# Splitting the first 256-token block of the feed-forward part, and rounding its weights earlier, in a fused top-k attention and SwiGLU kernel

## The chip, the cores and the metric

The kernel runs on one core of a Trainium2 chip. The metric is the device time of one execution in microseconds; the time before is the median of three runs. The profile is of one execution, taken by the hardware profiler. Its engines: PE (matrix multiply; PEld is its weight load), DVE, ACT, POOL, and SP, which here only issues DMAs.

## The reference

Attention over 8 batches x 8 heads, 576 tokens of 64 elements, in which each query keeps its 32 largest scores; then a gated feed-forward layer (512 to 1536 to 512) over all 4608 tokens. The three weight matrices lie in memory as 8-byte numbers; the kernel loads them as pairs of 32-bit words and makes fp32 of them itself.

```python
scores = scale * np.matmul(q, k.transpose(0, 1, 3, 2))
kth = np.partition(scores, -top_k, axis=-1)[..., -top_k:-top_k + 1]
scores = np.where(scores >= kth, scores, -1000000000.0)
attn = np.exp(scores - max); attn = attn / (sum + 1e-09)
x = np.matmul(attn, v)            # then (B,H,S,D) -> (4608, 512)
g = x @ w_gate
silu = g * (1.0 / (1.0 + np.exp(-g)))
return (silu * (x @ w_val)) @ w_out
```

## The kernel before, in words

**Units.** Attention is cut into 160 units (`units`, L227): batch, query tile of 128 tokens (five per batch, the last of 64), pair of heads. Four units, one per head pair, finish one query tile. Every fifth group of four is a short one ("J" below: `units[n][1] == J`, units 16 to 19, 36 to 39 and so on), with half the work. The loop at L514 is software-pipelined over units: in its pass n, DVE selects the top 32 of unit n (`select`, L257: four rounds of MAX8, L270, and three of MATCH_REPLACE8, L274, then the mask, L280), PE makes the scores of unit n+1 (`scores`, L234), turns the weights of unit n-1 (`turn`, L317) and multiplies unit n-2 by its values (`values`, L338). Unit n below means pass n of that loop, and it begins with the first MAX8 on `sc`.

**Order.** The order of each engine's instructions is exactly the order in which this Python text emits them (L570 to L583 add a dependency from each to the one before it). So an instruction that waits holds back all that was emitted behind it on its engine.

**Feed-forward blocks.** `values` copies its result into `xT[kb]`, a block of 256 tokens, and counts in `done`. When a block is full, `feed` (L396) turns it into pieces: 24 calls of eight matmul records each (`product`, L404 to L419; a call is one of 12 row groups of the gate or of the value matrix; each fp32 matmul shows as two records), then 12 calls of four records each for the second matmul (L440 to L460). After every second call of `product`, ACT and POOL instructions are queued (`gate`, `value`) and flushed later. That makes 36 pieces a block, 18 blocks, 648 pieces. A block of 256 tokens is full after eight ordinary units, so block 0 can start in pass 9 (the values of unit 7 come in pass 9), block 1 in pass 17.

**Credit.** `pieces(n)` (L493) emits up to n pieces, if a block is full and there is credit. Each pass adds 4.6 credits (2.3 in a J pass), capped at 8; a piece costs 1. A pass calls pieces(2), (1), (1), (1) and (6), at fixed places between the attention's instructions. After the loop, `while piece()` (L564) emits what is left.

**Rounding.** `weights` (L135) cuts the three weight matrices into 72 tiles of 128x256. Step k of this generator, in this order, finishes tile k-5 (DVE, L130), works on tile k-4 (DVE L120 and L123, then POOL L127), begins tile k-3 (POOL L108, ACT L113 and L115) and starts the load of tile k (SP, L102). There are 77 steps. `rounding(m)` emits m steps; `need(n)` (L160), called before matmuls, emits steps until n tiles are finished. Before the loop three steps are emitted. In the loop, each pass emits rounding(2) (rounding(1) from pass 10), then (1), (1), (1), at four places between the DVE's rounds of selection; so five steps a pass, four from pass 10 on.

Of the kernel before, what the change touches and what calls it, by code (L numbers as in the profile page):

```python
# [8 lines left out]
AF = mybir.ActivationFunctionType  # L9
# [6 lines left out]
P = 128  # L16
# [4 lines left out]
BLK = 256  # L21
# [6 lines left out]
def kernel(  # L28
# [27 lines left out]
    nc = tc.nc  # L56
    B, H, S, D = q.shape
    DM, DFF = w_gate.shape
    J = S // P
    JP = J * P  # L60
    R = S - JP
    NHP = H // 2
    KC = DM // P
    MC = DFF // P
    MS = MC // 2
    NBLK = B * S // BLK
    scale = 1.0 / float(D) ** 0.5
    assert D == 64 and R == 64 and H * D == DM and DM == 512 and B * S % BLK == 0

# [86 lines left out]
    def rounding(n):  # L156
        for _ in range(n):
            next(weight, None)

    def need(n):  # L160

        while ready[0] < n:
            next(weight)
# [63 lines left out]
    units = [(b, qt, hp) for b in range(B) for qt in range(J + 1) for hp in range(NHP)]  # L227
# [105 lines left out]
                yield  # L333
        state[n]["et"] = et

    xT, done = {}, {}

    def values(n):  # L338

        b, qt, hp = units[n]  # L340
        vt, v_last, vl = vs[b * NHP + hp]
        et = state.pop(n)["et"]
        last = qt == J
        ql = R if last else P
        av = ps_t.tile([P, P], FP32, tag="t", name="av")
        if not last:
            nc.tensor.matmul(av[:], vl[:], et[:, J, :], start=True, stop=False)
        for c in range(J + 1 if last else J):
            kl = R if c == J else P
            for hh in range(2):  # L350
                moving = (
                    et[0:kl, c, hh * R : (hh + 1) * R]
                    if last
                    else et[:, c + hh * (J + 1), :]
                )
                nc.tensor.matmul(  # L356
                    av[hh * R : (hh + 1) * R, 0:ql],
                    v_last[:, hh, :] if c == J else vt[:, hh, c, :],
                    moving,
                    start=last and c == 0,  # L360
                    stop=c == (J if last else J - 1),
                )
        c0 = b * S + qt * P
        at = c0
        while at < c0 + ql:
            kb = at // BLK
            n_c = min((kb + 1) * BLK, c0 + ql) - at
            if kb not in xT:
                xT[kb] = ffn.tile([P, NHP, BLK], FP32, tag="xT", name="xT", bufs=3)
                done[kb] = 0  # L370
            nc.scalar.copy(  # L371
                xT[kb][:, hp, at - kb * BLK : at - kb * BLK + n_c],
                av[:, at - c0 : at - c0 + n_c],
            )
            done[kb] += n_c
            at += n_c

    def store(o, g0):

        at = g0  # L380
        while at < g0 + P:
            b, c = divmod(at, S)
            j, p0 = divmod(c, P)
            n = min(g0 + P - at, S - c, P - p0)
            r0 = b * S + (c if j == J else J * p0 + j)
            dst = out[r0 : r0 + n, :] if j == J else out[r0 : r0 + J * (n - 1) + 1 : J, :]
            nc.sync.dma_start(dst, o[at - g0 : at - g0 + n, :])
            at += n

    on_act, on_pool = [], []  # L390

    def flush(queue):
        while queue:
            queue.pop(0)()

    def feed(kb):  # L396

        x = xT.pop(kb)
        hs = []

        def product(w, s, then):  # L404
            ps = ps_f.tile([P, 2, BLK], FP32, tag="f", name="f")
            need(8 * s + (4 if w is wg else 8))
            for i in range(2):
                m = 2 * s + i
                for c in range(KC):
                    nc.tensor.matmul(  # L410
                        ps[:, i, :],
                        w[:, c, m * P : (m + 1) * P],
                        x[:, c, :],
                        start=(c == 0),
                        stop=(c == KC - 1),
                    )
                if i == 1:
                    on_act.append(lambda: then(ps))
                yield  # L419

        for s in range(MS):
            h = ffn.tile([P, 2, BLK], FP32, tag="h", name="h", bufs=MS + 1)
            hs.append(h)


            def gate(ps, h=h):
                half = ffn.tile([P, 2, BLK], FP32, tag="gv", name="half_g", bufs=3)
                nc.scalar.activation(h[:], ps[:], AF.Tanh, scale=0.5)  # L428
                nc.scalar.mul(half[:], ps[:], 0.5)
                nc.scalar.add(h[:], h[:], 1.0)  # L430
                on_pool.append(lambda: nc.gpsimd.tensor_mul(h[:], h[:], half[:]))  # L431

            def value(ps, h=h):
                val = ffn.tile([P, 2, BLK], FP32, tag="gv", name="val", bufs=3)
                nc.scalar.copy(val[:], ps[:])  # L435
                on_pool.append(lambda: nc.gpsimd.tensor_mul(h[:], h[:], val[:]))  # L436

            yield from product(wg, s, gate)
            yield from product(wv, s, value)
        for t in range(BLK // P):  # L440
            ps = ps_f.tile([P, DM], FP32, tag="f", name="o_ps")
            for m in range(MC):
                need(8 * MS + 2 * m + 2)
                nc.tensor.matmul(  # L444
                    ps[:],
                    hs[m // 2][:, m % 2, t * P : (t + 1) * P],
                    wo[:, m, :],
                    start=(m == 0),
                    stop=(m == MC - 1),
                )  # L450
                if m == MC - 1:

                    def finish(ps=ps, t=t):
                        o = ffn.tile([P, DM], FP32, tag="o", name="o")
                        nc.scalar.copy(o[:], ps[:])
                        store(o, kb * BLK + t * P)

                    on_act.append(finish)
                if m % 2 == 1:
                    yield  # L460

    NU = len(units)
    todo = list(range(NBLK))
    current = []

    def piece():

        if len(on_act) > 1:
            flush(on_act)
        if len(on_pool) > 1:  # L470
            flush(on_pool)
        while True:
            if not current:
                if not todo or done.get(todo[0], 0) < NHP * BLK:
                    return False
                flush(on_act)
                flush(on_pool)
                current.append(feed(todo.pop(0)))
            if next(current[0], 0) == 0:
                current.pop()  # L480
                continue
            return True

    def fetch(n):

# [5 lines left out]
            load(i + NHP)  # L491

    def pieces(n):  # L493
        for _ in range(n):
            if credit[0] >= 1 and piece():
                credit[0] -= 1

    def run(steps):
        for _ in steps:
# [12 lines left out]
    credit = [0.0]  # L512
    no = iter(())
    for n in range(NU + 3):  # L514
        on = 0 <= n < NU
        was = 0 <= n - 1 < NU
        first = n < 2 * NHP + 2
        topk = select(n) if on else no
        over = normalize(n - 1) if was else no
        nxt = scores(n + 1) if n + 1 < NU else no  # L520
        over_et = turn(n - 1) if was else no
        ahead = fetch(n + 2) if n + 2 < NU else no
        if on:
            credit[0] = min(credit[0] + (2.3 if units[n][1] == J else 4.6), 8.0)
        flush(on_act)
        if was:
            penalize(n - 1)
            weigh(n - 1)
        flush(on_pool)
        if 0 <= n - 2 < NU:  # L530
            values(n - 2)
            b, qt, hp = units[n - 2]
            if qt == J and b + 1 < B:
                load_v((b + 1) * NHP + hp)
        next(topk, None)
        next(topk, None)
        rounding(2 if first else 1)
        next(topk, None)
        next(topk, None)
        rounding(1)  # L540
        pieces(2)
        next(over, None)
        flush(on_act)
        next(over, None)
        flush(on_pool)
        next(nxt, None)
        next(topk, None)
        rounding(1)
        pieces(1)
        next(nxt, None)  # L550
        flush(on_act)
        flush(on_pool)
        next(over_et, None)
        pieces(1)
        next(over_et, None)
        next(topk, None)
        rounding(1)
        next(topk, None)
        next(topk, None)
        next(ahead, None)  # L560
        pieces(1)
        next(ahead, None)
        pieces(6)
    while piece():  # L564
        pass
# [48 lines left out]
```

## Time and profile before

| what | number |
|---|---|
| median of three runs (lowest to highest) | 2067.86 us (2063.32 to 2073.43) |
| the profiled execution: its time, its span | 2063.52 us, 2061.4 us |
| PE busy, share of the span | 1854.4 us, 90% |
| DVE busy | 1673.8 us, 81% |
| ACT, POOL busy | 1150.5 us, 777.8 us |
| chain that ended last: PE, DVE, ACT | 77%, 11%, 6% |

The page cuts the span into 40 slices of about 51.5 us and gives the busy tenths of each engine in each. The trace answers for any stretch how long each engine was busy in it, with the granted PE clock (1.00 is full), and lists instructions in order of time with what ended the idle time before each.

### The profile page before, as it was taken

Reading aid. Unit: us, or ns where it says so; the run is one execution under the profiler, and the core shown is the slowest. Engines: PE = TensorE matmul, PEld = TensorE weight load, DVE = VectorE, ACT = ScalarE, POOL = GpSimd, SP = SyncE. Lnnn points to the kernel's source line nnn. Section 1 sums busy time; section 2 is a strip of 40 time slices with the busy share of each in tenths; the row PEclk is TensorE's granted clock in tenths of the full one; section 3 lists DMA queues with packets and bytes.
Section 4 is the critical chain, followed back from the end, with each engine's and each line's share of the span. In section 5 each row is a group of like instructions: output and inputs, shape, how many; then the busy total and the mean of one; then the engine's idle time right before and its main releaser. Section 6 shows DMA issues by size and latency. Waiting matters only on the chain.

```text
span 2061.4 us, 28952 instructions
## 1 busy us (share of the span) xinstructions
PE 1854.4 (90%) x9888; PEld 1276.5 (62%) x9888; DVE 1673.8 (81%) x3712; ACT 1150.5 (56%) x2565; POOL 777.8 (38%) x686
## 2 busy tenths in 40 slices
PE   3447779979999998899999999999999998999999
PEld 1325536657576766475757675757576766575756
DVE  5998986898789987989788987898788997989710
ACT  3555555656565655565656565656565655565621
POOL 2555543325333533242424342424333433242412
PEclk9657989989999999999999999999999999999999
DMA  5321111100020001100030002100020001000000
GB/s 149 88 77 62 62 33 49 33 6 1 19 64 11 1 13 43 38 1 11 9 74 1 11 2 58 24 11 1 19 64 11 1 12 42 17 1 11 1 11 11
DMA packets 111251, 59.55 MB, mean 29 GB/s; under 512 B 89088, under 2 KB 97280, under 8 KB 111104
## 3 DMA queue, kind: packets, MB, share of 16 engines
q1 hardware_dynamic: 111104, 57.70, 10.5%
q8 instruction: 79, 1.29, 0.3%
q14 instruction: 68, 0.56, 0.1%
HBM read 48.23 MB, written 9.44 MB: 28 GB/s over the span
## 4 chain that ended last, share of the span: by engine, by line
PE 77%; DVE 11%; ACT 6%; issue 3%; POOL 2%; SPq 1%; DMA 0%; POOLq 0%; DVEq 0%; ACTq 0%
PE f L410 35%; PE o_ps L444 18%; PE av L356 7%; PE etps L327 6%; PE s L250 5%; DVE m L270 4%; DVE rest L274 3%; ACT et L328 2%; PE s L251 2%; PE kqps L219 2%; DVE bits L123 1%; ACT e L315 1%; PE s L242 1%; DVE e L280 1%; POOL bits L127 1%
## 5 line engine op out<-in xcount | busy, mean ns | idle before, releaser
L270 DVE MAX8 m<-rest 128x8 f32<-128x576 f32 x864 | 613.6, 748 | 2.2
L292 POOL TENSOR_TENSOR e<-e,sc 128x1152 f32<-128x1152 f32 (+1 forms) x160 | 382.1, 2388 | 422.9 <-DVE e L280 307.7
L274 DVE MATCH_REPLACE8 rest<-m,rest 128x576 f32<-128x576 f32 x576 | 424.5, 745 | 0.0
L410 PE MATMUL f<-xT,wg 128*128 128x256 f32 x1728 | 413.0, 387 | 5.4 <-ACT xT L371 5.4
L444 PE MATMUL o_ps<-wo,h 128*128 128x512 f32 x864 | 407.5, 605 | 8.5 <-DVE wo L130 8.5
L410 PE MATMUL f<-xT,wv 128*128 128x256 f32 x1728 | 412.2, 385 | 0.0
L410 PEld LDWEIGHTS f<-xT,wg 128*128 128x128 f32 x1728 | 318.7, 192 | 57.4 <-issue 10.9
L410 PEld LDWEIGHTS f<-xT,wv 128*128 128x128 f32 x1728 | 321.5, 192 | 43.5 <-issue 3.4
L327 PE MATMUL etps<-ident,e 128*128 128x128 f32 (+1 forms) x1312 | 211.2, 290 | 132.2 <-issue 85.9
L431 POOL TENSOR_TENSOR h<-h,half_g 128x512 f32<-128x512 f32 x108 | 138.7, 1284 | 474.4 <-ACT h L430 474.4
L328 ACT COPY et<-etps 128x512 f32<-128x512 f32 (+1 forms) x448 | 196.3, 480 | 209.8 <-PE etps L327 209.7
L327 PEld LDWEIGHTS etps<-ident,e 128*128 128x128 f32 (+1 forms) x1312 | 164.8, 147 | 210.2 <-issue 136.3
L270 DVE MAX8 m<-sc 128x8 f32<-128x576 f32 x288 | 205.8, 752 | 85.7 <-ACT sc L246 42.0
L301 ACT ACTIVATE e<-e,bias 128x576 f32<-128x576 f32 x288 | 221.4, 773 | 81.3 <-POOL e L292 81.3
L444 PEld LDWEIGHTS o_ps<-wo,h 128*128 128x128 f32 x864 | 153.2, 192 | 150.2 <-issue 137.8
L436 POOL TENSOR_TENSOR h<-h,val 128x512 f32<-128x512 f32 x108 | 138.8, 1285 | 236.6 <-ACT val L435 236.3
L315 ACT ACTIVATE e<-e,tot 128x576 f32<-128x576 f32 x288 | 209.0, 771 | 19.2 <-DVE tot L312 19.2
L274 DVE MATCH_REPLACE8 rest<-m,sc 128x576 f32<-128x576 f32 x288 | 212.2, 745 | 0.0
L356 PE MATMUL av<-et,v 128*64 128x128 f32 (+1 forms) x2560 | 199.9, 284 | 8.7 <-ACT et L328 4.5
L356 PEld LDWEIGHTS av<-et,v 128*64 128x64 f32 x2560 | 150.7, 146 | 45.1 <-ACT et L328 22.6
L428 ACT ACTIVATE h<-f 128x512 f32<-128x512 f32 x108 | 64.4, 596 | 166.7 <-PE f L410 166.4
L250 PE MATMUL s<-kqT 64*128 64x512 f32 x512 | 153.1, 676 | 2.0 <-ACT kqT L224 2.0
(51 smaller groups left out, 1517.5 us busy)
## 6 DMA issues: line engine op xcount, KB each, us to landing
kq_in<-in_k_dram SPq DMA_DIRECT2D x64, 128.0 KB, 2.8
kq_in<-in_q_dram SPq DMA_DIRECT2D x64, 128.0 KB, 2.9
v<-in_v_dram SPq DMA_DIRECT2D x32, 256.0 KB, 3.1
w<-in_moe_w_gate_dram SPq DMA_DIRECT2D x24, 256.0 KB, 2.7
w<-in_moe_w_val_dram SPq DMA_DIRECT2D x24, 256.0 KB, 2.7
w<-in_moe_w_out_dram SPq DMA_DIRECT2D x24, 256.0 KB, 2.5
out_dram<-o SPq DMA_DIRECT2D x40, 128.0 KB, 2.4
out_dram<-o SPq DMA_DIRECT2D x16, 256.0 KB, 2.3
```

The costliest lines, as they stand in the source:

```text
L250: nc.tensor.matmul(ps[:, 1024 * hh : 1024 * hh + JP], slab[d, qs], slab[d, 0:JP])
L270: nc.vector.max(m[:, t, 8 * r : 8 * r + 8], cur[:, hs])
L274: nc.vector.match_replace(rest[:, hs], m[:, t, 8 * r : 8 * r + 8], cur[:, hs], LOWEST)
L292: nc.gpsimd.tensor_tensor(e[:, every], e[:, every], sc[:, every], ALU.add)
L301: nc.scalar.activation(e[:, hs], e[:, hs], AF.Exp, bias=bias[:, t : t + 1], scale=scale, accum_out=tot[:, t : t + 1],)
L315: nc.scalar.mul(e[:, hs], e[:, hs], tot[:, t : t + 1])
L327: nc.tensor.transpose(ps[0:kl, c * P : (c + 1) * P], e[:, k0 : k0 + kl], ident[:])
L328: nc.scalar.copy(et[0:kl, c0 : c0 + cn, :], ps[0:kl, 0 : cn * P].rearrange("p (c j) -> p c j", c=cn),)
L356: nc.tensor.matmul(av[hh * R : (hh + 1) * R, 0:ql], v_last[:, hh, :] if c == J else vt[:, hh, c, :], moving, start=last and c == 0, stop=c ...
L410: nc.tensor.matmul(ps[:, i, :], w[:, c, m * P : (m + 1) * P], x[:, c, :], start=(c == 0), stop=(c == KC - 1),)
L436: on_pool.append(lambda: nc.gpsimd.tensor_mul(h[:], h[:], val[:]))
L444: nc.tensor.matmul(ps[:], hs[m // 2][:, m % 2, t * P : (t + 1) * P], wo[:, m, :], start=(m == 0), stop=(m == MC - 1),)
```

## The change

The first block of 256 tokens becomes two of 128 (`blocks`). Their `product` calls have 128 columns instead of 256, take half a credit each, and the ACT and POOL instructions behind them are half as wide; the second half of a block, 12 calls for 256 tokens, is six calls for each of the two. All other blocks are as before. `pieces(n)` now counts in credits and not in calls, so that pieces(2) emits four half calls, and pieces(6) up to twelve. The cap on credit goes from 8.0 to 10.0. The rounding goes from 5 steps a pass to 7 in passes 0 to 5 (as 3, 1, 1 and 2 at the four places), is 5 in passes 6 to 9 (2, 1, 1, 1) and 4 after that.

```diff
-    NBLK = B * S // BLK
+    blocks = [(0, P), (P, P)] + [(g, BLK) for g in range(BLK, B * S, BLK)]
...
-            kb = at // BLK
-            n_c = min((kb + 1) * BLK, c0 + ql) - at
+            kb = at // BLK + 1 if at >= P else 0
+            g0, size = blocks[kb]
+            n_c = min(g0 + size, c0 + ql) - at
...
+        g0, size = blocks[kb]
+        c = slice(0, size)
+        cost = size / BLK
...
-                        ps[:, i, :],
-                        w[:, c, m * P : (m + 1) * P],
-                        x[:, c, :],
+                        ps[:, i, c],
+                        w[:, kc, m * P : (m + 1) * P],
+                        x[:, kc, c],
...
-                yield
+                yield cost
...
-                nc.scalar.activation(h[:], ps[:], AF.Tanh, scale=0.5)
+                nc.scalar.activation(h[:, :, c], ps[:, :, c], AF.Tanh, scale=0.5)
...
-        for t in range(BLK // P):
+        for t in range(size // P):
...
     def pieces(n):
-        for _ in range(n):
-            if credit[0] >= 1 and piece():
-                credit[0] -= 1
+        while n > 0 and credit[0] >= 1:
+            size = piece()
+            if not size:
+                break
+            n -= size
+            credit[0] -= size
...
-        first = n < 2 * NHP + 2
+        first = 2 if n < NHP + 2 else 1 if n < 2 * NHP + 2 else 0
...
-            credit[0] = min(credit[0] + (2.3 if units[n][1] == J else 4.6), 8.0)
+            credit[0] = min(credit[0] + (2.3 if units[n][1] == J else 4.6), 10.0)
...
-        rounding(2 if first else 1)
+        rounding(1 + first)
...
-        rounding(1)
+        rounding(1 + first // 2)
```

More of the change, by code (lines that the diff above doesn't have):

```diff
@@ L334, in turn @@
         state[n]["et"] = et
-    xT, done = {}, {}
+    xT, done = {}, [0] * len(blocks)
     def values(n):
@@ L365, in values @@
         while at < c0 + ql:
-            kb = at // BLK
-            n_c = min((kb + 1) * BLK, c0 + ql) - at
+            kb = at // BLK + 1 if at >= P else 0
+            g0, size = blocks[kb]
+            n_c = min(g0 + size, c0 + ql) - at
             if kb not in xT:
                 xT[kb] = ffn.tile([P, NHP, BLK], FP32, tag="xT", name="xT", bufs=3)
-                done[kb] = 0
             nc.scalar.copy(
-                xT[kb][:, hp, at - kb * BLK : at - kb * BLK + n_c],
+                xT[kb][:, hp, at - g0 : at - g0 + n_c],
                 av[:, at - c0 : at - c0 + n_c],
@@ L408, in product @@
                 m = 2 * s + i
-                for c in range(KC):
+                for kc in range(KC):
                     nc.tensor.matmul(
-                        ps[:, i, :],
-                        w[:, c, m * P : (m + 1) * P],
-                        x[:, c, :],
-                        start=(c == 0),
-                        stop=(c == KC - 1),
+                        ps[:, i, c],
+                        w[:, kc, m * P : (m + 1) * P],
+                        x[:, kc, c],
+                        start=(kc == 0),
+                        stop=(kc == KC - 1),
                     )
@@ L427, in gate @@
                 half = ffn.tile([P, 2, BLK], FP32, tag="gv", name="half_g", bufs=3)
-                nc.scalar.activation(h[:], ps[:], AF.Tanh, scale=0.5)
-                nc.scalar.mul(half[:], ps[:], 0.5)
-                nc.scalar.add(h[:], h[:], 1.0)
-                on_pool.append(lambda: nc.gpsimd.tensor_mul(h[:], h[:], half[:]))
+                nc.scalar.activation(h[:, :, c], ps[:, :, c], AF.Tanh, scale=0.5)
+                nc.scalar.mul(half[:, :, c], ps[:, :, c], 0.5)
+                nc.scalar.add(h[:, :, c], h[:, :, c], 1.0)
+                on_pool.append(
+                    lambda: nc.gpsimd.tensor_mul(h[:, :, c], h[:, :, c], half[:, :, c])
+                )
             def value(ps, h=h):
                 val = ffn.tile([P, 2, BLK], FP32, tag="gv", name="val", bufs=3)
-                nc.scalar.copy(val[:], ps[:])
-                on_pool.append(lambda: nc.gpsimd.tensor_mul(h[:], h[:], val[:]))
+                nc.scalar.copy(val[:, :, c], ps[:, :, c])
+                on_pool.append(
+                    lambda: nc.gpsimd.tensor_mul(h[:, :, c], h[:, :, c], val[:, :, c])
+                )
             yield from product(wg, s, gate)
             yield from product(wv, s, value)
-        for t in range(BLK // P):
+        for t in range(size // P):
             ps = ps_f.tile([P, DM], FP32, tag="f", name="o_ps")
@@ L455, in finish @@
                         nc.scalar.copy(o[:], ps[:])
-                        store(o, kb * BLK + t * P)
+                        store(o, g0 + t * P)
                     on_act.append(finish)
                 if m % 2 == 1:
-                    yield
+                    yield 1
     NU = len(units)
-    todo = list(range(NBLK))
+    todo = list(range(len(blocks)))
     current = []
@@ L473, in piece @@
             if not current:
-                if not todo or done.get(todo[0], 0) < NHP * BLK:
-                    return False
+                if not todo or done[todo[0]] < NHP * blocks[todo[0]][1]:
+                    return 0
                 flush(on_act)
@@ L478, in piece @@
                 current.append(feed(todo.pop(0)))
[L479 to L482, printed above, removed]
+            size = next(current[0], 0)
+            if size:
+                return size
+            current.pop()
     def fetch(n):
```

## The prediction

> **What bounds the kernel now.** I read the page's 40 slices first: PE is busy 3 to 7 tenths in the first eight slices and 9 nearly everywhere after, so the beginning is the only part with room on PE. Then I asked for the busy times stretch by stretch, cut at the beginnings of units (the first MAX8 on `sc` in the list of instructions). Columns: stretch and length, then busy us (count) of PE, PEld, DVE, ACT, POOL, then granted clock, DMA share, GB/s.
>
> ```profile
> 121.35:172.85 51.50, 22.40 (x101) 14.51 (x100) 47.21 (x119) 27.12 (x67) 26.61 (x36) 0.60 0.26 77
> 172.85:191.56 18.71, 15.06 (x66) 11.18 (x66) 16.02 (x41) 10.46 (x25) 9.65 (x12) 0.80 0.22 71
> 191.56:212.98 21.42, 18.61 (x101) 14.66 (x100) 15.31 (x37) 12.73 (x29) 12.94 (x15) 1.00 0.16 50
> ...
> 267.28:291.62 24.34, 15.85 (x54) 7.60 (x53) 19.40 (x47) 10.14 (x26) 10.97 (x17) 0.82 0.10 35
> ...
> 302.38:310.31 7.93, 7.41 (x44) 3.82 (x42) 6.25 (x14) 4.91 (x11) 2.83 (x2) 1.00 0.11 37
> ```
>
> ```profile
> 427.65:449.18 21.53, 12.37 (x66) 8.73 (x66) 21.46 (x49) 11.12 (x26) 5.62 (x4) 0.74 0.01 2
> ```
>
> The first row is units 6 to 8: 17.17 us each, DVE busy 15.74, PE less than half. The last is units 27 and 28, which have neither rounding nor feed-forward pieces: 10.77 us each, all DVE. So early units are bound by DVE: 10.77 of selection plus five steps of rounding; units 9 to 14 carry rounding and the 36 pieces of block 0 together. From unit 17 on a unit takes the larger of DVE's 10.77 (6.3 in a J unit) and PE's sum.
>
> How a step is paid shows in DVE's list of instructions, in unit 14, where `need` emits steps one right behind another:
>
> ```profile
> 276.76 0.41 DVE L130 SCALAR_TENSOR_TENSOR wo<-size,bits 128x256 f32<-128x256 f32 x1
> 277.09 0.28 DVE L120 TENSOR_SCALAR bits<-hi 128x256 int32<-128x256 int32 x1
> 277.40 0.43 DVE L123 SCALAR_TENSOR_TENSOR bits<-hi,bits 128x256 int32<-128x256 int32 x1
> 278.77 0.62 DVE L130 SCALAR_TENSOR_TENSOR wo<-size,bits 128x256 f32<-128x256 f32 x1 [0.94 <-POOL bits L127]
> 279.31 0.28 DVE L120 TENSOR_SCALAR bits<-hi 128x256 int32<-128x256 int32 x1
> 279.63 0.42 DVE L123 SCALAR_TENSOR_TENSOR bits<-hi,bits 128x256 int32<-128x256 int32 x1
> 280.98 0.62 DVE L130 SCALAR_TENSOR_TENSOR wo<-size,bits 128x256 f32<-128x256 f32 x1 [0.93 <-POOL bits L127]
> ```
>
> A step that stands alone between rounds of selection costs DVE 1.00 us ((15.74 - 10.73) / 5). A step right behind another costs 2.21 (278.77 to 280.98): DVE waits for POOL's addition of the step before. In units 1 to 8 the one pair a unit, rounding(2), costs 3.40 (106.96 to 110.36 in the same list); 10.77 + 3.40 + 3 x 1.00 = 17.17, the unit's length.
>
> The prices on PE are in the end of the chain of work that ended last:
>
> ```profile
> 1994.96 41.44 PE f L410 x192
> 2036.40 20.61 PE o_ps L444 x48
> ```
>
> A `product` call is 41.44 / 24 = 1.73 us, a call of the second matmul 20.61 / 12 = 1.72. The attention's own PE work is 12.37 x 0.74 / 2 = 4.6 a unit at full clock; I take 4.5.
>
> **The change, part by part.** I counted pieces and steps per pass by the code's credit rule, for both kernels; for before, the counts agree with the records in the trace (36 pieces in passes 9 to 16: 8, 4, 5, 4, 5, 4, 5, 1). After, passes 5 to 7 emit 9.5, 4.5 and 4 credits of pieces, pass 8 none, passes 9 to 11 again 9.5, 4.5, 4, passes 12 to 16 none, since block 1 is full only in pass 17. The total by pass 16 is the same 36. The steps: 7 a pass in 0 to 5, then `need` pulls the rest forward: 17 in pass 6, 15 in pass 7, where all 77 are spent.
>
> *Unit 0*: in before, DVE stands until 32.66 us for the load of the fourth weight tile. After, that wait sits one place earlier in DVE's order, so a pair of MATCH_REPLACE8 (1.5) and two more steps (1.0 + 2.2) follow it: **+4.7**.
>
> *Units 1 to 5*: a run of three (3.40 + 2.21), two single steps, a pair (3.40): 10.77 + 11.0 = 21.8 against 17.17: **+23.2** for five. PE in unit 5 has 4.5 plus 19 half calls. A half call: records with 128x128 weights and 128 columns follow each other every 0.11 us where several stand in a row (five in the turning of `e`), so 8 x 0.109 = 0.87, and unit 5 is 21 us of PE, hidden by 21.8 of DVE. The other bound: PEld's mean is 192 ns per load in L410; if loads can't overlap each other, 1.54 a call and 33.8 us, which shows. I take 0.87, the nearest row.
>
> [...]
>
> *Units 6 to 8*: the forced steps stand in runs. Unit 6: a pair (3.4), a run of six (3.4 + 4 x 2.21 = 12.3), a run of eight (3.4 + 6 x 2.21 = 16.7), one single: 44.2. Unit 7: a pair, a run of five (10.0), a run of eight that ends in steps with no new tile (16.0): 40.2. Unit 8 has nothing: 10.8. To that I add 3 us (bounds 0 and 12) for waits through the queues: in runs, POOL's additions stand behind feed-forward multiplications which wait for ACT, and these for PE's half calls, which wait for the weights; in before's unit 10, DVE's L130 waited up to 4.4 us for POOL that way. 98.2 against 51.5: **+46.7**. Loads aren't what limits: 256 KB every 2.21 us is 119 GB/s, and the first stretch of the trace moved 149.
>
> *Units 9 to 16*: no steps are left, so DVE needs 10.77 a unit (before: 137.5 us for the eight, 172.85 to 310.31). But half the pieces now fall into units 9 to 11 where nothing of DVE's hides them: PE needs 4.5 + 19 x 0.87 = 21.1, then 4.5 + 5 x 0.87 + 2 x 1.72 = 12.3, and 8.4 up to the scores of unit 12. With 2 us for a slow clock at the start of the burst (in before, the first 16 records took 4.68 us instead of 3.65) and a copy on ACT that is 45. Then units 12 to 15 at 10.77 and unit 16 at 6.3: 94.4: **-43.1**. ACT's and POOL's instructions for the block are half as wide and twice as many; both engines are idle for half of these units and hide it; without that cover it would be some 5 us of ACT.
>
> So unit 17 begins 4.7 + 23.2 + 46.7 - 43.1 = **31.5 us later**.
>
> *From unit 17 on* only the cap acts: a block that starts after a starved stretch starts with 10 credits, not 8. Units 17 to 37: unit 17, a J unit with 4 pieces before, gets 10, +6 x 1.73 = 10.4; units 23 and 25 lose 1 and 5, of which PE's bound gives back 4.2 (units 25 and 26 can't fall below 10.77); unit 29 +3.5; units 35 to 37 +1.1. Around units 63 to 73, and again 143 to 153: two starts at +3.5 each, less the 2.2 or so that units 63, 71 and 72 (12.16, 11.35, 10.94 long) have above 10.77: +4.7 each time. Units 107 to 117: +3.2. At the end 44 pieces instead of 46 remain after the last unit: -3.5. Sum **+19.9**. If PE is not what these units wait for, it is 0, and at most it is 25.
>
> Total 31.5 + 19.9 = +51.4 on the profiled execution's 2063.5 (span 2061.4 and 2.1 around it): **2115 us**. The median of the runs shown lies 4.3 higher, inside their spread of 10.
>
> **The rivals.**
>
> *Half calls cost as much as the load, 1.54.* For: PEld's 192 ns. Against: 0.11 us between records. Units 9 and 10 grow by 24 x 0.67 = 16, unit 5 shows some 8: 2130 to 2140. Chance 0.12.
>
> *The larger bursts cost nothing*, since PE catches up in the units after. For: unit 26 takes 12.7 with PE busy 10.7. Against: unit 30 is 18.4 us long with PE busy throughout. Then 2063.5 + 31.5 = 2095. Chance 0.15.
>
> *Runs of steps go at the price of single ones* (the pipeline fills, or POOL's wait falls on work that DVE has anyhow). The count of steps that directly follow another is 43 (3 in each of passes 0 to 5, 13 and 12 in 6 and 7); at 1.0 instead of 2.2 that takes off 52: 2063, no change. Against: the seven lines above. Chance 0.06.
>
> *Faster*: the same, and the bursts free as well, so that the earlier pieces really leave the path: units 9 to 16 shed what PE made DVE wait in them. 2063 - 20 = 2043. It decides when idle time of DVE before L130 falls below 0.5 us per step in a run. Chance 0.05.
>
> **How the numbers follow.** The forecast has 0.62, with 2100 to 2130 as its own range. The range 2085 to 2150 takes in the forecast, the free bursts, the dear half calls and the bounds of the waits through queues; below it lie no change and faster (0.11), above it dear half calls and long queue waits together. Slower by over 0.5% (10 us, about what a measurement of this kernel can tell from no change): 0.89; within: 0.06; faster: 0.05.
>
> **What would show it.** Right: units 1 to 5 at about 21.8 us, units 6 and 7 over 40 with DVE's idle time before L130 named POOL; units 12 to 16 without records of L410; unit 17 about 20 us; PE busy tenths lower in slices 5 to 7 of 40 than before, and the last 44 pieces after the last unit. Wrong: units 6 and 7 under 30 us, half calls at 1.5 us, or unit 17 beginning before 325 us in the span.

## The result, and the profile after

The changed kernel takes 2133.04 us (median of four runs, 2130.98 to 2139.85), against 2065.88 for the kernel before in the same set of runs: a ratio of 1.0325, 95% interval 1.0288 to 1.0361. It is slower by 67 us. The profiled execution took 2130.98 us with a span of 2129.2, 67.8 more than before's.

The page's slices of the changed kernel, of 53.2 us each:

```profile
PE   2454687988989999999999999999999998999999
...
DVE  5876777798968897879778987897868996979720
...
PEclk6576697998999999999999999999999999999999
```

The same rows of the kernel before, in slices of 51.5 us:

```profile
PE   3447779979999998899999999999999998999999
...
DVE  5998986898789987989788987898788997989710
```

DVE, which bounds the beginning, reads 8, 7, 6, 7, 7 in slices 2 to 6, where before had 9, 9, 8, 9, 8: it stands still more, and has the same work (1670.8 us busy against 1673.8). PE shows its earlier pieces in slice 3 (5, before 4), but reads 4, 6, 8 in slices 4 to 6, where before had 7, 7, 7, and 7 in slice 7, where before had 9; the granted clock is down to 7 there, in the units without pieces. (In before's row, PE is at 3 to 7 in the first six slices, and not in the first eight, as the prediction has it.) The busy times by unit, with the columns of the prediction's first view (units 3; 5; 6; 7; 10; 12 to 15; 17 and 18):

```profile
83.94:105.86 21.92, 6.93 (x36) 4.96 (x37) 18.56 (x46) 10.51 (x27) 11.12 (x17) 0.59 0.29 84
127.78:152.56 24.78, 18.48 (x108) 17.09 (x109) 18.52 (x46) 13.07 (x36) 12.86 (x19) 0.77 0.28 81
152.56:205.47 52.91, 31.52 (x160) 22.04 (x158) 31.27 (x77) 22.75 (x62) 28.60 (x46) 0.68 0.27 85
205.47:245.15 39.68, 20.68 (x34) 7.47 (x35) 27.70 (x69) 14.88 (x39) 18.31 (x29) 0.57 0.21 67
266.68:290.48 23.80, 23.80 (x194) 20.91 (x193) 11.05 (x25) 12.42 (x34) 10.41 (x13) 1.00 0.00 1
301.24:344.29 43.05, 27.94 (x149) 18.36 (x149) 42.91 (x98) 22.64 (x50) 11.24 (x8) 0.76 0.03 8
352.11:382.47 30.36, 30.13 (x164) 24.28 (x163) 12.39 (x27) 12.27 (x25) 10.42 (x9) 0.91 0.04 12
```

The first row's stretch is unit 3 alone, and so on to the last, which holds units 17 and 18, two short J units that took 19.3 us before. In units 6 and 7, DVE is idle for 21.6 and 12.0 us. What ended that idle time, from the waits of DVE in unit 6 (who, for whom: us in all, times, longest):

```profile
DVE wo L130 <- POOL bits L127: 7.9, 7, 2.4
DVE wg L130 <- POOL bits L127: 7.8, 2, 6.9
DVE wv L130 <- POOL bits L127: 5.0, 4, 2.2
```

Nearly all of it is L130, the instruction that waits for POOL's addition. The single wait of 6.9 us is far more than the 0.93 of an ordinary pair of steps: in DVE's list, L123 of a step begins at 156.0 and L130 of the next at 163.79, and in POOL's the addition in between (L127) had to wait behind feed-forward multiplications and the attention's L290 and L292.

```profile
159.50 0.73 POOL L435 TENSOR_TENSOR h<-h,half_g 128x256 f32<-128x256 f32 x1 [1.23 <-ACT h L433]
160.29 0.21 POOL L290 TENSOR_SCALAR bias<-m 128x2 f32<-128x2 f32 x1
160.46 2.61 POOL L292 TENSOR_TENSOR e<-e,sc 128x1152 f32<-128x1152 f32 x1
163.03 0.72 POOL L127 TENSOR_TENSOR bits<-bits,ulps 128x256 int32<-128x256 int32 x1
```

POOL's multiplication waited for ACT's L433, and ACT for PE, which was still working off unit 5's half calls; the rounding stood in the same queue. The end of the chain: 8 + 24 + 12 calls after the last unit, where before had 10 + 24 + 12 (its first line is the first one here, the other two are in the prediction).

```profile
1975.87 19.09 PE o_ps L444 x40
```

```profile
2047.16 15.63 PE o_ps L451 x32
2062.79 41.44 PE f L413 x192
2104.23 20.61 PE o_ps L451 x48
```

### The profile page after: what moved, and what is told of

It is laid out like the page before. It is cut to its first block, busy times and chain, and to the rows that moved or that the text cites. A ratio compares the mean times of both kernels' runs of the same rounds, so it can differ in the third digit from the quotient of the medians.

```text
span 2129.2 us, 29485 instructions
## 1 busy us (share of the span) xinstructions
PE 1881.3 (88%) x10080; PEld 1299.3 (61%) x10080; DVE 1670.8 (78%) x3712; ACT 1154.8 (54%) x2589; POOL 773.4 (36%) x698
## 4 chain that ended last, share of the span: by engine, by line
PE 75%; DVE 13%; ACT 6%; POOL 3%; issue 2%; SPq 1%; DMA 0%; POOLq 0%; ACTq 0%
PE f L413 36%; PE o_ps L451 17%; PE av L356 6%; PE etps L327 6%; PE s L250 5%; DVE m L270 5%; DVE rest L274 4%; ACT et L328 2%; PE s L251 2%; PE kqps L219 2%; POOL bits L127 1%; DVE bits L123 1%; ACT e L301 1%; POOL e L292 1%; PE s L242 1%
## 5 line engine op out<-in xcount | busy, mean ns | idle before, releaser
L292 POOL TENSOR_TENSOR e<-e,sc 128x1152 f32<-128x1152 f32 (+1 forms) x160 | 382.0, 2388 | 524.2 <-DVE e L280 407.1
L451 PE MATMUL o_ps<-wo,h 128*128 128x512 f32 x864 | 415.5, 614 | 27.4 <-DVE wo L130 27.4
L413 PE MATMUL f<-xT,wg 128*128 128x256 f32 (+1 forms) x1824 | 416.0, 376 | 19.3 <-ACT xT L371 11.8
L413 PE MATMUL f<-xT,wv 128*128 128x256 f32 (+1 forms) x1824 | 418.4, 377 | 5.5 <-DVE wv L130 5.5
L413 PEld LDWEIGHTS f<-xT,wg 128*128 128x128 f32 x1824 | 329.6, 195 | 66.3 <-ACT xT L371 14.7
L413 PEld LDWEIGHTS f<-xT,wv 128*128 128x128 f32 x1824 | 327.9, 194 | 51.5 <-issue 7.0
L435 POOL TENSOR_TENSOR h<-h,half_g 128x512 f32<-128x512 f32 (+1 forms) x114 | 138.6, 1216 | 437.3 <-ACT h L433 437.2
L442 POOL TENSOR_TENSOR h<-h,val 128x512 f32<-128x512 f32 (+1 forms) x114 | 139.7, 1225 | 249.1 <-ACT val L440 249.0
L356 PE MATMUL av<-et,v 128*64 128x128 f32 (+1 forms) x2560 | 206.7, 289 | 9.0 <-ACT et L328 4.5
L311 DVE TENSOR_SCALAR tot<-tot 128x2 f32<-128x2 f32 (+1 forms) x160 | 25.8, 161 | 215.3 <-ACT e L301 214.4
L356 PEld LDWEIGHTS av<-et,v 128*64 128x64 f32 x2560 | 156.1, 148 | 46.3 <-ACT et L328 23.2
## 6 DMA issues: line engine op xcount, KB each, us to landing
kq_in<-in_k_dram SPq DMA_DIRECT2D x64, 128.0 KB, 2.9
kq_in<-in_q_dram SPq DMA_DIRECT2D x64, 128.0 KB, 3.0
out_dram<-o SPq DMA_DIRECT2D x40, 128.0 KB, 2.4
```

The lines of the kernel that those rows point to most:

```text
L292: nc.gpsimd.tensor_tensor(e[:, every], e[:, every], sc[:, every], ALU.add)
L356: nc.tensor.matmul(av[hh * R : (hh + 1) * R, 0:ql], v_last[:, hh, :] if c == J else vt[:, hh, c, :], moving, start=last and c == 0, stop=c ...
L413: nc.tensor.matmul(ps[:, i, c], w[:, kc, m * P : (m + 1) * P], x[:, kc, c], start=(kc == 0), stop=(kc == KC - 1),)
L442: lambda: nc.gpsimd.tensor_mul(h[:, :, c], h[:, :, c], val[:, :, c])
L451: nc.tensor.matmul(ps[:], hs[m // 2][:, m % 2, t * P : (t + 1) * P], wo[:, m, :], start=(m == 0), stop=(m == MC - 1),)
```

## The experiments

Theory: the loss has three parts. The early start forces rounding steps into runs, where DVE waits for POOL; it leaves PE without pieces in units 12 to 16; and the cap of 10 makes larger bursts where PE bounds. The rivals: the cost is in the seven early steps, in the half-width calls, or the cap is free. Eleven kernels, in three sets; each ratio is to the kernel before on the same chip, with its 95% interval. In us, a ratio is multiplied by some 2067. What is told by unit comes from one profiled execution of each kernel.

**1. The cap alone** (kernel before).

```diff
-            credit[0] = min(credit[0] + (2.3 if units[n][1] == J else 4.6), 8.0)
+            credit[0] = min(credit[0] + (2.3 if units[n][1] == J else 4.6), 10.0)
```

> The kernel before with only the cap on credit raised from 8 to 10. My theory (a larger burst costs PE 1.73 us a piece wherever a block starts after a starved stretch, and gives little back where units are at DVE's 10.77): +3.4 at unit 9, -1.7 at unit 16, +3.4 at 17, -1 at 25, then +3.5, +1.1, +4.7, +3.2, +4.7 and -3.5 at the end: about +18 us, 2081 on the profiled execution. The rival (bursts are free): within 4 us of before. A second rival, that only the end counts: -3.5 us.

Measured: 2084.4, 1.0084 (1.0057 to 1.0111), +17 us. The bursts are not free, and the sum over units was right to a microsecond or two. Unit 10 of this kernel:

```profile
191.16:214.64 23.48, 22.18 (x118) 17.80 (x117) 15.42 (x37) 13.22 (x30) 14.29 (x16) 1.00 0.13 46
```

It is 2.1 us longer than before's (21.42, third row of the prediction's first view), and PE is busy 3.6 us more: the two pieces more.

**2. The rounding schedule alone** (kernel before, 7 steps a pass in passes 0 to 5).

```diff
-        first = n < 2 * NHP + 2
+        first = 2 if n < NHP + 2 else 1 if n < 2 * NHP + 2 else 0
...
-        rounding(2 if first else 1)
+        rounding(1 + first)
...
-        rounding(1)
+        rounding(1 + first // 2)
```

> The kernel before with only the rounding changed (7, then 5, then 4 steps a pass; whole first block, cap 8). My theory (a step right behind another costs 2.2 us, one alone 1.0): units 0 to 5 grow by 4.6 + 5 x 4.75 = 28; unit 13 loses 4 single steps (-4.6) and unit 14 its eight, six of them in a run (-11.9): +11 us, 2075. The rival (rounding early is moved work and costs nothing in sum): -5 to 0 us, since unit 14's forced run goes away.

Measured: 2077.07, 1.0036 (1.0015 to 1.0057), +7 us (3 to 12). Units 1 to 5 took 21.93 us, as worked out; units 13 and 14 gave back a little more than thought (unit 14: 10.76). The expected 11 lies inside the interval; "nothing in sum" doesn't.

**3. The split and the cap, with the rounding schedule of before.** The edit of run 2, backwards, on the changed kernel.

> The changed kernel with the rounding schedule of before (5 steps a pass at first), so that the split and the cap stand alone. My theory: the first half block then forces 12 more steps in a run inside unit 5, at 2.2 us each, and units 0 to 4 are as short as before: unit 0 -4.6, units 1 to 4 -19, unit 5 +18 to +21, the rest as in the changed kernel: 2125 to 2131, so the seven steps are not what costs, the split is. The rival (the seven early steps are the cost, 28 us of it): 2100 to 2105.

Measured: 2130.27, 1.0305 (1.0275 to 1.0335). The seven steps are not the cost; without them the changed kernel is nearly as slow. Units 1 to 4 are back at 17.17, and unit 5, which now forces twelve steps, takes 51.37 us instead of 24.78.

**4. The changed kernel with the stages of a step further apart.** The absolute value (`size`) moves into the second stage, with three buffers; in all it is two steps more, and the sum of the work is the same. The two lines that set the distances:

```diff
-            for lag in (5, 4, 3, 0):
+            for lag in (7, 5, 3, 0):
...
-            ready[0] = max(n - 4, 0)
+            ready[0] = max(n - 6, 0)
```

> The changed kernel with the rounding's stages set further apart (a tile's second stage two steps behind its first and its third two behind the second, in place of one; two steps more in all, and the absolute value is taken in the second stage), so that a step right behind another need not wait for POOL's result of the step before. My theory (the 43 adjacent steps each lose 1.2 us to that wait): adjacent steps fall to 1.1 to 1.3 us, -40 us, about 2091. The rival (a run of steps is bound by POOL's or ACT's own rate, or by the loads, not by the wait from step to step): units 6 and 7 stay over 40 us each, 2125 to 2135.

Measured: 2112.96, 1.0223 (1.0197 to 1.0248): 20 us off, half of what the theory said, and clear of the rival. The instructions of DVE and POOL in unit 6 show why:

```profile
177.18 0.41 DVE L130 SCALAR_TENSOR_TENSOR wo<-size,bits 128x256 f32<-128x256 f32 x1
177.40 0.77 POOL L127 TENSOR_TENSOR bits<-bits,ulps 128x256 int32<-128x256 int32 x1 [0.43 <-ACT size L117]
177.69 0.63 DVE L120 TENSOR_SCALAR bits<-hi 128x256 int32<-128x256 int32 x1
178.14 0.45 POOL L108 TENSOR_SCALAR hi<-w 128x256 f32<-128x256 f32 x1
178.35 0.52 DVE L123 SCALAR_TENSOR_TENSOR bits<-hi,bits 128x256 int32<-128x256 int32 x1
178.80 0.41 DVE L130 SCALAR_TENSOR_TENSOR wo<-size,bits 128x256 f32<-128x256 f32 x1
```

The wait before L130 is gone in this run of steps, and a step follows the last after 1.62 us instead of 2.21. But it isn't the 1.1 to 1.3 expected: L120 takes 0.63 beside POOL's addition where it takes 0.28 alone. Over units 0 to 7, DVE's idle time before L130 falls from 50.6 us to 6.3, but DVE is busy for 187.6 us instead of 168.4, 17 of the 19 more in L120. So the wait of a step on the step before was real, and behind it stands a second bound that the prediction did not have: L120 gets longer beside POOL's addition.

**5. The changed kernel with the cap at 8.**

> The changed kernel with the cap on credit back at 8. My theory (the cap's cost stands by itself, as the run with only the cap raised showed, 17 us): 2113 or so. The rival (the larger cap is what makes the early start pay, so that with 8 the changed kernel is no better or worse): 2128 and more.

Measured: 2102.48, 1.0161 (1.0135 to 1.0188). The cap costs 31 us here by the medians (34 by the ratios, 25 between the two profiled executions), not the 17 that it costs alone. In its profiled execution unit 17 begins 9.5 us earlier than in the changed kernel (342.56 against 352.11): units 6 to 8 take 5.9 us less and unit 10 takes 4.0 less, with smaller bursts from passes 5 and 9, which the expected figure left out.

**6. The split alone, started late**: the blocks of the changed kernel, but no piece before pass 9, with before's rounding and cap.

```diff
-                if not todo or done[todo[0]] < NHP * blocks[todo[0]][1]:
+                if not todo or at_pass[0] < 2 * NHP + 1 or done[todo[0]] < NHP * blocks[todo[0]][1]:
```

> The split alone, started late: two blocks of 128 at first, but no piece before pass 9, with the rounding and the cap of before. Credits spent per pass are those of before from pass 12 on, and the forced steps fall into passes 11 and 12 with about 13 steps right behind another, against 6 in before's pass 14. My theory (half-width calls cost what they should, 0.89 us; the cost is where the early start puts the steps and the pieces): +5 to +12 us, 2069 to 2076. The rival (halving the width is itself what costs, by twice as many instructions on PE, ACT and POOL): over 2085.

Measured: 2071.98, 1.0016 (0.9998 to 1.0034). Half-width calls are not what costs; this is no change, or 3 us. Its unit 11 carries the run of steps and takes 41.5 us, but before's long unit 14 is gone in turn (11.36 us instead of 24.34), and the starved units don't exist in it.

**7. The split alone, started early**: the changed kernel with before's rounding and before's cap (the edits of runs 3 and 5 together).

> The changed kernel with the rounding schedule and the cap of before, so that the split with its early start stands alone. My theory (the parts add, with the cap worth 29 us in the changed kernel and the seven steps about nothing, as the runs without each of them showed): 2130 - 29 = about 2101. The rival (the early start costs little by itself, as the late split did, and what costs is its meeting with the cap): 2075 to 2085.

Measured: 2101.75, 1.0151 (1.0123 to 1.0179). The early start by itself costs 31 us; with the cap it is 63 (run 3), and with the seven steps as well 67. The parts don't simply add: 31 and the 17 of the cap alone make 48. Units 5, 6 and 7 of this kernel:

```profile
104.17:136.53 32.36, 23.04 (x153) 20.02 (x153) 21.53 (x52) 17.42 (x47) 17.00 (x24) 0.82 0.22 66
136.53:184.36 47.83, 27.28 (x125) 21.49 (x123) 32.13 (x77) 20.17 (x54) 25.41 (x42) 0.57 0.34 100
184.36:232.13 47.77, 22.14 (x40) 7.61 (x35) 33.38 (x82) 19.73 (x52) 24.51 (x39) 0.60 0.32 99
```

DVE is busy in 87.0 of 128.0 us there, PE in 72.5 and no engine else in more. Of DVE's 41 idle us, 38.4 stand before L130, waiting for POOL's addition. So waits bound it there, and no engine's rate. The loads run at 99 to 100 GB/s in units 6 and 7, where the first slice of the kernel before moves 149. No run takes the starved units 12 to 16 away and keeps the early start, so what they cost by themselves is not shown.

**8. Six single steps a pass, none next to each other** (kernel before, `rounding(1)` at six places in every pass until the 77 are spent; two of the places are new, behind the first and behind the last MAX8 pair).

> The kernel before with six single rounding steps a pass at six places between DVE's rounds of selection, until the 77 are done, and none next to each other. My theory (the wait of a step on the one before it is what is lost): no idle time of DVE before L130, units 1 to 8 at 16.8 us with a step more each, no forced run in unit 14: -18 us, about 2046. The rival (DVE waits for POOL wherever the steps stand): 2060 to 2066.

Measured: 2071.12, 1.0014 (0.9999 to 1.0029): no gain, and my theory of single steps at 1.00 us failed here. Units took 19.05 us, and DVE was busy in 18.8 of them. The timeline in unit 4:

```profile
94.86 0.40 DVE L130 SCALAR_TENSOR_TENSOR wv<-size,bits 128x256 f32<-128x256 f32 x1
94.92 3.01 POOL L292 TENSOR_TENSOR e<-e,sc 128x1152 f32<-128x1152 f32 x1
95.19 0.28 DVE L120 TENSOR_SCALAR bits<-hi 128x256 int32<-128x256 int32 x1
95.50 2.72 DVE L123 SCALAR_TENSOR_TENSOR bits<-hi,bits 128x256 int32<-128x256 int32 x1
```

L123, 0.43 us elsewhere, takes 2.72: it begins while POOL's L292 runs, and ends 0.29 us after it.

**9. The same with the cap at 6.**

> As the run with six single steps a pass, and the cap on credit at 6 in place of 8. My theory (smaller bursts spread the pieces over units that DVE holds at 10.77 anyway): by the same sum over units that gave 16.5 us for a cap of 10 against 8, a cap of 6 gives 19.5 us less: about 2027. The rival (pieces left out of the burst come back after the last unit, 48 in place of 46, and what is saved elsewhere is lost again): 2045 to 2050.

Measured: 2061.27, 0.9959 (0.9946 to 0.9973). A smaller cap is worth 10 us against run 8, half of the 19.5 worked out. That it is worth something is shown; where the other half stays isn't. One trace suggests a part: unit 20 takes 12.51 us here, at a granted clock of 0.73, against 11.11 at 1.00 in run 8.

**10 and 11. Six single steps, the first behind the first MATCH_REPLACE8 pair instead**, with a cap of 8, and of 6.

```diff
-        rounding(2 if first else 1)
+        rounding(1)
         next(topk, None)
+        rounding(1)
         next(topk, None)
...
         rounding(1)
         next(topk, None)
+        rounding(1)
         next(topk, None)
         next(ahead, None)
```

> The kernel before with six single rounding steps a pass as in the run that spread them before, but with the first of them behind the first MATCH_REPLACE8 and not behind the first MAX8 (and one behind the second MAX8 instead). The theory formed from that run's trace: its first step of each pass stood beside POOL's 2.6 us addition of L292, and DVE's L123, which reads two operands from SBUF, took 2.72 us instead of 0.43 until that addition ended; with the step later the units come down from 19.05 to 16.8 us, twelve of them: -25 us against that run, about 2046. The rival (each step in a pass of six costs 1.34 us wherever it stands): 2066 to 2072 again.

> The same with the cap on credit at 6. The earlier pair of runs showed 10 us between a cap of 8 and of 6 (I had worked out 19.5): 2036. The rival (that difference came from the colliding step, not from the cap): 2044 to 2048.

Measured: 2060.35, 0.9960 (0.9943 to 0.9977), and 2046.72, 0.9899 (0.9879 to 0.9919). The later place is worth 11 us, not 25: units take 17.85 instead of 19.05, and still not 16.8, because L292 now meets the step's L130, which takes 1.48 us. The second was put at 2036, and its time lies in the range of its rival, by which the cap would have done nothing in runs 8 and 9; but it is 13.6 us below the first, which differs from it in the cap alone, so that rival's reason fell. What missed is the price of the steps, as in the first. The second is also the fastest kernel of the study, 21 us below before, and goes the other way in every part of the change: a whole first block, no steps side by side, a smaller cap. Units 4 and 10 of it:

```profile
89.72:107.58 17.86, 6.68 (x37) 4.78 (x35) 17.62 (x43) 9.79 (x25) 9.45 (x14) 0.60 0.30 88
198.79:219.57 20.78, 16.42 (x87) 12.46 (x87) 20.14 (x43) 12.54 (x31) 13.57 (x17) 0.92 0.25 76
```

Six steps now fit into about the time of five, and in unit 10 rounding and pieces share the unit, with DVE busy almost throughout.

## Why the prediction was right, and where it was mis-sized

Slower was right, and the time lay within the range of 2085 to 2150, 18 us above the forecast and 3 above the 2100 to 2130 that the forecast had as its own. It falls among the 2130 to 2140 of the rival of dear half calls, so the time alone would have spoken for that rival; what decides against it are the records. By the terms of the sum, in us, the time of the profiled executions by beginnings of units:

| term | forecast | measured |
|---|---|---|
| unit 0 | +4.7 | +4.6 |
| units 1 to 5 | +23.2 | +26.6 (four at 21.92, unit 5 at 24.78) |
| units 6 to 8 | +46.7 | +51.9 (52.9, 39.7, 10.8) |
| units 9 to 16 | -43.1 | -41.3 (unit 16: 7.8, put at 6.3) |
| unit 17 begins later by | 31.5 | 41.8 |
| from there to unit 159 | +23.4 | +32.9 |
| the end | -3.5 | -6.9 |

*The price of adjacent steps* held: runs of steps in units 6 and 7 follow each other at 2.2 us, as in before's unit 14. That the cause is the wait for POOL is shown by run 4, which takes 44 us of it away and wins 20; most of the rest went into DVE's own instructions, which were busy for 19 us more beside POOL's.

*Unit 5* failed by 3 us. PE did not bound it: it was busy for 18.5 of the 24.8 us, at a granted clock of 0.77. DVE waited before L130 for 5.7 us, where the run of three and the pair have 2.8 (three times 0.93). The prediction had put the waits through the queues at something in units 6 to 8 and at nothing here, but they begin with the first half calls: POOL's addition stood behind a multiplication that waited for ACT.

```profile
149.18 0.62 DVE L130 SCALAR_TENSOR_TENSOR wv<-size,bits 128x256 f32<-128x256 f32 x1 [2.96 <-POOL bits L127]
```

```profile
147.74 0.73 POOL L435 TENSOR_TENSOR h<-h,half_g 128x256 f32<-128x256 f32 x1 [2.46 <-ACT h L433]
```

The price of a half call, 0.87, was right where PE had its full clock (1.00 granted from 152.56 to 160.00 us): in the burst at the start of unit 6, sixteen records begin every 1.79 us, 0.89 a call. The rival of 1.54 a call is out, and run 6 agrees.

```profile
154.68 1.95 PE L413 MATMUL f<-xT,wv 128*128 128x128 f32 x16
156.47 1.95 PE L413 MATMUL f<-xT,wg 128*128 128x128 f32 x16
```

*Unit 6* failed by 5.7: the queues' waits, put at 3 with bounds of 0 and 12, were 8.6. Three waits before L130 took 6.86, 2.36 and 2.19 us where an ordinary pair has 0.93, the longest behind PE's backlog, as shown above. The bounds held that, the value taken was too low; unit 7 gave back 0.5.

*From unit 17 on* the term was too small, by 9.5 us up to unit 159, of which 3.4 came back after it. "Only the cap acts" was not right either: with the cap at 8 (run 5), the changed kernel still takes 10 us more than before from there to the end, and the cap of 10 adds 16. The starved units leave a full credit in any case, so pass 17 emits 8 pieces with a cap of 8 and 10 with one of 10, where before emits 4; the forecast's number for unit 17 has this, its words don't. The cap alone was summed to a microsecond (run 1). A part of the 9.5 may be dips of the granted clock in the stretch of J units, as in unit 40 (12.57 us at 0.73, where before had 10.75 at 1.00); run 10, which has before's pieces in that unit, shows such a dip as well (13.61 at 0.75), so it does not take the moved pieces to make one. How much of the 9.5 this makes is open.

*The rival that ends faster* fell with its own condition: idle time before L130 did not drop below 0.5 us a step, it was 20.7 us over the 17 steps of unit 6, 1.2 a step. "The runs go at the price of single ones" fell as well, and "the bursts are free" with run 1.

*The signs* that the prediction named held for the most part: units 1 to 4 at 21.9, DVE's idle time named POOL, no record of L413 (before's L410) in units 12 to 16, 44 pieces at the end. Three failed in the letter. Unit 7 took 39.7 us, just under the 40 named. Unit 17 took 11.15 us and not 20, because DVE runs ahead of PE there: the burst shows in unit 18 (19.21), and the two together are 11.1 us longer than before, against 10.4 worked out. And PE is not lower in all of slices 5 to 7: it reads 6, 8, 7, where before had 7, 7, 9.

The gain that the early start could have had went to the units without pieces. PE got 18 of the 36 pieces four passes earlier, but block 1 needs units 8 to 15 as before, so nothing that follows can begin earlier; units 12 to 15 stand without pieces at DVE's 10.77, and unit 16 at 7.8; the pieces they might have hidden were emitted in passes 9 to 11, and PE bounds there (unit 10: 23.80 us, PE busy throughout).

## What to carry to other kernels

Before work is moved forward in a pipeline, look up what it needs: here the first block's second product needs all 72 weight tiles, so starting it four passes early turned single steps, hidden among other work, into runs in which one engine waits for another at every step. Count then what the moved work leaves behind: if the next block's inputs come no earlier, the time won at the front becomes idle time in the middle. And a limit on how much work may be saved up is worth trying smaller where the saved-up work comes out as a burst on the engine that bounds: here 10 was slower than 8, and 8 slower than 6.

## What the runs showed of the hardware

Some of DVE's instructions and of POOL's took longer beside each other than alone. In run 8, L123 took 2.72 us beside POOL's L292 and 0.43 otherwise, and ended 0.29 after it; the 64 L123 between 36 and 250 us of that run take from 0.42 to 2.73 us, 0.43 in the median. In the traces of the kernel before and of the changed one together, each of the 49 L123 and L130 that begin with more than 0.2 us of a POOL instruction to go ends 0.28 to 0.29 us after that one, and takes 0.62 to 1.38; the 20 that begin alone, and during which a POOL instruction begins, take 0.42 to 0.43. L130 took 1.48 beside L292 (run 10) and 0.41 alone. POOL's take longer as well: its L108 takes 0.64 us where DVE's L130 began 0.05 us before it, and 0.41 in the median otherwise (kernel before). L120 took 0.63 beside POOL's L127 (run 4) and 0.28 alone; in run 8 it takes 0.28 in the middle of L292, and L292 3.01 instead of the 2.62 of run 10. MAX8 and MATCH_REPLACE8 take 0.73 to 0.77 us beside any of them, and as much alone. What makes the others longer, no run here shows. The prediction did not count with it: it priced a step that stands alone at DVE's own time, 1.00 us.
